# Cross-attention into a gated MLP on one Trainium2 core: one x load on another queue, the first output taken in pairs and partly ahead of the next scores, and fewer stores in the last group

## The chip, the core and the metric

The kernel runs on one core of a Trainium2 chip. The core has a matrix engine (TensorE, called PE in the profile, with its weight loads as PEld), three engines for elementwise work (VectorE = DVE, ScalarE = ACT, GpSimd = POOL) and SyncE (SP), which here only issues DMAs. PE writes to PSUM banks; DVE and ACT empty them into SBUF. DMAs are issued from the queues of SP, ACT and POOL. The metric is the time of one execution on the device, in microseconds; less is better.

## What is computed

The reference, cut to what matters:

```python
def _attn_ref(x, state):                      # x (8, 8, 512, 64), state (8, 8, 32, 64)
    scale = 1.0 / np.sqrt(D)
    scores = scale * np.matmul(x, state.transpose(0, 1, 3, 2))
    a = softmax(scores)                       # over the 32 state rows
    xread = np.matmul(a, state)
    scores2 = scale * np.matmul(state, x.transpose(0, 1, 3, 2))
    a2 = softmax(scores2)                     # over the 512 tokens
    sread = np.matmul(a2, x)
    return np.concatenate([xread, sread], axis=2)

def _moe_ref(x, w_gate, w_val, w_out):        # 512 -> 1536 -> 512
    gate = 1.0 / (1.0 + np.exp(-(x @ w_gate)))
    val = x @ w_val
    return (gate * val) @ w_out
```

The attention's 8 heads of 64 are joined to 512 columns, and every one of the 8 x 544 rows goes through the MLP. In the reference each softmax takes the maximum off first and adds 1e-9 to the sum; the kernel takes the exponential of the scaled scores alone.

## The kernel before

Work goes by batch: 8 batches of 512 tokens, and a ninth group of 256 rows that holds the 32 state rows of all batches (`b == B`). Matrix operands are bf16, sums fp32. xread is never formed: state times the gate and value weights (`SW`, by `sw_mm`) comes first, and the softmax weights, transposed (`aT`), multiply it.

For one batch the steps are these, each with its helper:

- `load_x` (L70): x of the batch, 1 MB of fp32, into one of three `xf` buffers. `cast_x` (L96) makes bf16 of it; from batch 2 on POOL does that.
- `at_xT_dma` (L121): four DMA transposes from SP's queue make `xT`.
- `S_mm` (L126), twice: 8 matmuls each, scores of half the heads into a PSUM bank. `S_exp` (L132): ACT's exponential, which frees that bank. `n_sum`, `n_mul` (L146, L167): sum, reciprocal and product on DVE. `aT_dma` (L190): four DMA transposes from SP's queue.
- `sw_wide` (L253), twice: 32 matmuls for half of the 1536 columns of SW of the batch, into OU, AT and four banks of SWP; `sw_cp` (L271) moves them to SBUF on ACT or DVE.
- `gv_mm` (L278), 12 times: gate and value of 128 columns into the two GV banks; `gv_th` (ACT's tanh) and `gv_glu` (DVE) make `glu`.
- `out_mm` (L308), 12 times: a token chunk c of 128 (four chunks) needs 12 matmuls against `wo`, in three groups of four (f0 = 0, 4, 8). After the third group ACT writes the bank to `res`, one of three buffers, and SP stores it.
- `sr_mm`, `sr_inv`, `sr_fin` (L199 to L224): the state rows' read, into `XS`.

The PSUM banks are named by pool: AT and OU have one bank each, GV two, SWP four.

The order on each engine is the order in which the helpers are called; there is no scheduler. Lines 349 to 568 hold a prologue, written out by hand: loads, batches 0 and 1 up to their `glu`, casts and transposes of x of batches 2 and 3. In it x of batches 0 and 1 is loaded on SP's queue, most weights on POOL's, x of batch 2 on POOL's (L490), then three loads of `wo` (L491 to L493), and x of batch 3 on ACT's queue (L502).

Then the loop of L570 runs b from 1 to 8 over twelve steps f. In step f the output group f of batch b - 1 and, if b > 1, gate and value f of batch b run on PE, and the scores, SW and state read of batch nb = b + 1 are spread between. `v, q` (L580) tell which half of SW and which place in it a step has. For b = 1 gate and value are done, so the steps hold output groups of batch 0 alone, in the two GV banks, and the scores of batch 2 stand ahead of all steps (L572 to L578). After the loop come two chunks of the ninth group, with four stores each (L322 to L324), and chunk 3 of batch 7 in three pieces (`out_last`, L326), whose last store ends the program.

Of the kernel before, what the change touches and what calls it, by code (L numbers as in the profile page):

```python
# [8 lines left out]
FP = mybir.dt.float32  # L9
# [7 lines left out]
def kernel(  # L17
# [14 lines left out]
    nc = tc.nc  # L32
    B, H, S, D = x.shape
    Ns = state.shape[2]
    SC = S + Ns
# [7 lines left out]
    wp = ctx.enter_context(tc.tile_pool(name="wp", bufs=1))  # L43
# [3 lines left out]
    fp = ctx.enter_context(tc.tile_pool(name="fp", bufs=3))  # L47
# [22 lines left out]
    def load_x(b, eng, parts=1, hold=None):  # L70
        xf = stg.tile((128, H, 4, D), FP, name="xf")
        if hold is not None:

            hold.memset(xf[:, 0, 0, 0:1], 0.0)
        v = x[b].rearrange("h (p c) d -> p h c d", c=4)
        n = H // parts
        for i in range(parts):
            eng.dma_start(xf[:, n * i:n * i + n], v[:, n * i:n * i + n])
        xfs[b] = xf
# [2 lines left out]
        src = (moe_w_gate, moe_w_val)[w].rearrange("(k p) n -> p k n", p=128)  # L82
        nc.gpsimd.dma_start((wg, wv)[w][:, :, lo:lo + n], src[:, :, lo:lo + n])  # L83

    def gate():

        nc.gpsimd.tensor_copy(pre[:, 1:2], xfs[1][:, 0, 0, 0:1])

    def cast_w(w, cp):
        cp((wg, wv)[w][:, :, 0:256], wfs[w])  # L90
# [1 line left out]
    def load_wo(q):  # L92
        nc.gpsimd.dma_start(wo[:, 4 * q:4 * q + 4],
                            moe_w_out.rearrange("(k p) n -> p k n", p=128)[:, 4 * q:4 * q + 4])

    def cast_x(b, cp, lo, n):  # L96
        if b not in xbs:
            xbs[b] = xp.tile((128, 4, H, D), BF, name="xb")
        cp(xbs[b].rearrange("p c h d -> p h c d")[:, lo:lo + n], xfs[b][:, lo:lo + n])  # L99
# [26 lines left out]
    def S_mm(b, i, place):  # L126
        ps = held["S", b, i] = place[0].tile((128, 4, 2, 2, Ns), FP, name="Sp", tag=place[1])
        for jj in range(2):
            for c in range(4):
                nc.tensor.matmul(ps[:, c, :, jj], xTs[b][:, 2 * i + jj, c], sTz[:, b, 2 * i + jj], start=True, stop=True)  # L130

    def S_exp(b, i):  # L132
        if b not in E1s:
            E1s[b] = ap_.tile((128, 4, 2, 4, Ns), FP, name="E1")
        nc.scalar.activation(E1s[b][:, :, :, 2 * i:2 * i + 2].rearrange("p c e j n -> p (c e) j n"),  # L135
                             held["S", b, i].rearrange("p c e j n -> p (c e) j n"), AF.Exp, scale=scale)
# [9 lines left out]
    def n_sum(b, i):  # L146
        rs = ap_.tile((128, 8, 2), FP, name="rs")
        nc.vector.tensor_reduce(rs, halfE(b, i), AX.X, ALU.add)  # L148
        ri = held["ri", b, i] = ap_.tile((128, 8, 2), FP, name="ri")
        nc.vector.reciprocal(ri, rs)  # L150
# [16 lines left out]
    def n_mul(b, i, eng):  # L167
        if b not in abs_:
            abs_[b] = ap_.tile((128, 4, 2, 128), BF, name="ab")
        ri = held["ri", b, i]  # L170
        eng.tensor_tensor(abs_[b].rearrange("p c e (j n) -> p (c e) j n", n=Ns)[:, :, 2 * i:2 * i + 2], halfE(b, i),  # L171
                          ri.unsqueeze(3).to_broadcast((128, 8, 2, Ns)), ALU.mult)
# [17 lines left out]
    def aT_dma(b):  # L190
        for c in range(4):
            nc.sync.dma_start_transpose(aT_tile(b)[:, c], abs_[b][:, c].rearrange("p e k -> p (e k)"))
# [105 lines left out]
    def gv_glu(b, f):  # L298
        if b not in glus:
            glus[b] = fp.tile((128, NF, n_of(b)), BF, name="glu", bufs=2, padded_shape=(128, NF, 512))  # L300
        nc.vector.scalar_tensor_tensor(glus[b][:, f], held["th", b, f], 1.0, held["gv", b, f][1], ALU.add, ALU.mult)  # L301
# [5 lines left out]

    def out_mm(b, k):  # L308
        c, f0 = k // 3, (k % 3) * 4
        if f0 == 0:  # L310
            place = SWP if b == B else GV if b == 0 else OU
            ops[b, c] = place[0].tile((128, 512), FP, name="outp", tag=place[1])
        for f in range(f0, f0 + 4):
            nc.tensor.matmul(ops[b, c], glus[b][:, f, c * 128:(c + 1) * 128], wo[:, f],  # L314
                             start=(f == 0), stop=(f == NF - 1))
        if f0 == 8:
            res = fp.tile((128, 512), FP, name="res")
            nc.scalar.activation(res, ops[b, c], AF.Copy, scale=0.5)  # L318
            if b < B:
                nc.sync.dma_start(rows_of(b, c), res)  # L320
            else:
                for i in range(4):  # L322
                    r0 = (4 * c + i) * SC + S
                    nc.sync.dma_start(out[r0:r0 + Ns], res[i * Ns:(i + 1) * Ns])  # L324

    def out_last(b, c):  # L326

        res = fp.tile((128, 512), FP, name="res")
        for lo, n in ((0, 256), (256, 128), (384, 128)):
            cs = slice(lo, lo + n)  # L330
            ps = p_sw.tile((128, 512), FP, name="outp", tag="swp")[:, :n]
            for f in range(NF):
                nc.tensor.matmul(ps, glus[b][:, f, c * 128:(c + 1) * 128], wo[:, f, cs],  # L333
                                 start=(f == 0), stop=(f == NF - 1))
            if lo == 256:
                nc.scalar.activation(res[:, cs], ps, AF.Copy, scale=0.5)
                nc.scalar.dma_start(rows_of(b, c)[:, cs], res[:, cs])
            else:
                nc.vector.tensor_scalar(res[:, cs], ps, 0.5, None, op0=ALU.mult)
                nc.sync.dma_start(rows_of(b, c)[:, cs], res[:, cs])  # L340
# [8 lines left out]
    sf = wp.tile((128, 16, D), FP, name="sf")  # L349
    nc.sync.dma_start(sf, state.rearrange("b h (u l) d -> (b h u) l d", l=16))  # L350
    load_x(0, nc.sync, 2)
    load_x(1, nc.sync)
    wfs = []
    for src in (moe_w_gate, moe_w_val):
        wf = wp.tile((128, 4, 256), FP, name="wf", bufs=2)
        nc.sync.dma_start(wf, src.rearrange("(k p) n -> p k n", p=128)[:, :, 0:256])
        wfs.append(wf)
    make_identity(nc, ident)
    nc.vector.memset(sTz, 0.0)
    for e in range(2):  # L360
# [24 lines left out]
    def pad(b, n=1):  # L385
        for e in range(2):
            rows = slice(e * 64, (e + 1) * 64)
            nc.gpsimd.tensor_copy(sTz[rows, b:b + n, :, e], sTc[rows, b:b + n])

    cast_x(0, vec, 2, 2)  # L390
    cast_x(0, pool, 4, 2)
    cast_x(0, act, 0, 2)
# [11 lines left out]
    S_mm(0, 0, SWP)  # L404
    S_exp(0, 0)
    warm(12, SWP)
    gate()
    load_w(0, 256, 256)
    S_mm(0, 1, AT)
    cast_x(1, act, 4, 4)  # L410
# [80 lines left out]
    load_wo(0)  # L491
    load_wo(1)
    load_wo(2)  # L493
    gv_glu(0, 5)
    sw_cp(1, 512, 1, 1, vec)
    sw_visit(1, 512, 512, 0)
# [2 lines left out]
    sr_mm(1, AT)  # L499
    sw_cp(1, 512, 1, 0, vec)  # L500
    gv_mm(1, 1, GV)
    load_x(3, nc.scalar)  # L502
    gv_th(1, 1)
    sw_visit(0, 1024, 512, 0)
    sw_visit(0, 1024, 512, 1)
# [63 lines left out]

    for b in range(1, B + 1):  # L570
        nb = b + 1 if b + 1 < B else None
        if b == 1:  # L572
            for i in range(2):
                S_mm(nb, i, (AT, GV)[i])
                S_exp(nb, i)
                n_sum(nb, i)
                n_mul(nb, i, nc.vector)
            aT_dma(nb)  # L578
        for f in range(NF):
            v, q = f // 6, f % 6  # L580
            if nb is not None and q == 0:
                sw_wide(nb, v)
                sw_cp(nb, v, 0, 0, act)
                sw_cp(nb, v, 0, 1, act)
            for first in (nb is not None and q == 0, nb is None or q > 0):
                if first and b > 1:
                    gv_mm(b, f, SWP if b == B and f % 2 else GV)
                    gv_th(b, f)
                    gv_glu(b, f)
                elif not first and (b < B or f < 9):  # L590
                    out_mm(b - 1, f)
            if nb is not None:
                if q == 0:
                    sw_cp(nb, v, 1, 0, vec)
                elif q in (1, 3, 4):
                    k = {1: 3, 3: 4, 4: 5}[q]
                    sw_cp(nb, v, k // 2, k % 2, act)
                if f in (1, 2) and b > 1:
                    S_mm(nb, f - 1, AT)
                    S_exp(nb, f - 1)  # L600
                elif f in (6, 7):
                    n_tok(nb, f - 6)
                    if f == 7:
                        n_split(nb, 0)
                elif f == 8:
                    n_split(nb, 1)
                elif f == 9:
                    sr_mm(nb, AT)
                    sr_inv(nb)
                elif f == 10:  # L610
                    sr_fin(nb)
                if f in (2, 4) and b > 1:
                    n_sum(nb, f // 2 - 1)
                elif f in (3, 5) and b > 1:
                    n_mul(nb, f // 2 - 1, nc.vector)
                if f == 3:
                    at_Eb(nb)
                    if nb + 2 < B:
                        load_x(nb + 2, nc.sync)
                elif f == 5 and b > 1:  # L620
                    aT_dma(nb)
                    if nb + 1 < B:
                        cast_x(nb + 1, pool, 0, 4)
                        cast_x(nb + 1, pool, 4, 4)
                        at_xT_dma(nb + 1)
# [33 lines left out]
```

The softmax here doesn't subtract the row's maximum and nothing guards it: scores larger than these inputs give would overflow.

## Time and profile before

| what | us |
|---|---|
| median of 13 runs (lowest, highest) | 231.36 (230.74, 233.78) |
| the profiled execution's own time | 232.05 |
| its span, first to last instruction | 230.2 |
| PE busy in the span | 219.0 |
| DVE, ACT, POOL busy | 141.5, 131.3, 42.5 |
| x of batch 3, issue to landing | 15.6 |
| the three `wo` loads, issue to landing | 12.7, 16.8, 19.6 |

Times inside the span count from its start. A busy time is the union of an engine's instructions; a wait of one engine is put down to what ended it. The ends of matmuls are modelled, so distances between matmuls are best taken from start to start. In a timeline row the columns are start, length, engine, line, operation, what it writes and reads, shape, how many were merged, and in brackets the idle time before it with what ended it. "SPq" and "ACTq" are the DMA queues' issuing instructions. A DMA's landing is the time at which its completion shows.

### The profile page before, as it was taken

What the parts mean: (1) busy time and instruction counts of PE and PEld (TensorE: products, weight loads), DVE (VectorE), ACT (ScalarE), POOL (GpSimd) and SP (SyncE); (2) the same over time, 40 slices, a digit from 0 to 9 for tenths busy, and PEclk for the clock granted to TensorE, in tenths of its full rate; (3) what the DMA queues carried; (4) which work ended last, traced back from release to release, by engine and by line L of the source; (5) the groups of instructions that cost most, each with busy time, mean ns of one, the idle gap of its engine ahead of it and who ended that gap; (6) DMA issues with size and microseconds to landing.
All of it is one profiled execution on the core that took longest, in us unless ns stands there. A gap on an engine that the chain in (4) does not pass through costs nothing.

```text
span 230.2 us, 4759 instructions
## 1 busy us (share of the span) xinstructions
PE 219.0 (95%) x1856; PEld 113.0 (49%) x1856; DVE 141.5 (61%) x234; ACT 131.3 (57%) x246; POOL 42.5 (18%) x75
## 2 busy tenths in 40 slices
PE   7678999989899999999999999999999999999994
PEld 6563345444444444444444544454445444466744
DVE  2499889975339864886478747874687443332311
ACT  3587877655467566665675567655755544423311
POOL 1399820150006000600060006000200000000000
PEclk9889999999999999999999999999999999999999
DMA  6999999923658243724372441235122111111113
GB/s 214 354 154 195 227 272 241 176 49 80 163 215 257 54 80 114 231 80 81 117 217 85 82 126 46 68 75 133 46 65 74 47 46 48 47 69 67 49 30 107
DMA packets 38790, 28.09 MB, mean 122 GB/s; under 512 B 20976, under 2 KB 34160, under 8 KB 38768
## 3 DMA queue, kind: packets, MB, share of 16 engines
q1 hardware_dynamic: 32560, 21.44, 33.5%
q0 software_dynamic: 5024, 5.24, 12.9%
q10 hardware_dynamic: 1184, 1.11, 1.7%
q8 instruction: 14, 0.23, 0.4%
q14 instruction: 8, 0.07, 0.1%
HBM read 18.35 MB, written 8.91 MB: 118 GB/s over the span
## 4 chain that ended last, share of the span: by engine, by line
PE 77%; DMA 13%; SPq 3%; POOL 3%; ACT 1%; issue 1%; DVE 0%; POOLq 0%; ACTq 0%
PE outp L314 35%; PE gvp L286 29%; PE gvp L289 5%; PE swp L234 4%; DMA xf<-in_x_dram 4%; DMA wv<-in_moe_w_val_dram 4%; DMA out_dram<-res 4%; DMA xT<-xb 3%; SPq L124 2%; PE srp L211 1%; PE outp L333 1%; PE Sp L130 1%; POOL xb L99 1%; PE srp L208 1%; POOL wg L83 1%
## 5 line engine op out<-in xcount | busy, mean ns | idle before, releaser
L301 DVE SCALAR_TENSOR_TENSOR glu<-th,gvp 128x512 bf16<-128x512 f32 (+1 forms) x108 | 70.3, 657 | 65.4 <-ACT th L296 50.6
L314 PE MATMUL outp<-wo,glu 128*128 128x512 bf16 x396 | 97.7, 379 | 0.2 <-ACT res L318 0.2
L286 PE MATMUL gvp<-aT,SW 128*128 128x512 bf16 x384 | 96.4, 379 | 1.0 <-ACT res L318 0.9
L296 ACT ACTIVATE th<-gvp 128x512 f32<-128x512 f32 (+1 forms) x108 | 61.6, 575 | 62.2 <-PE gvp L286 51.4
L286 PEld LDWEIGHTS <-SW 128*128 128x128 bf16 x384 | 36.2, 98 | 46.1 <-issue 5.2
L314 PEld LDWEIGHTS <-glu 128*128 128x128 bf16 x396 | 37.5, 98 | 41.4 <-issue 0.9
L272 ACT CAST SW<-swp 128x512 bf16<-128x512 f32 (+1 forms) x78 | 42.2, 578 | 3.0 <-PE swp L234 1.6
L318 ACT ACTIVATE res<-outp 128x512 f32<-128x512 f32 x33 | 19.7, 597 | 21.3 <-PE outp L314 17.5
L141 POOL CAST Eb<-E 128x256 bf16<-128x256 f32 x32 | 12.4, 429 | 99.3 <-ACT E L135 99.3
L99 POOL CAST xb<-xf 128x1024 bf16<-128x1024 f32 (+1 forms) x13 | 14.6, 1147 | 21.5 <-DMA xf<-in_x_dram 16.5
L272 DVE CAST SW<-swp 128x512 bf16<-128x512 f32 x20 | 13.4, 684 | 2.9 <-PE swp L234 2.9
L171 DVE TENSOR_TENSOR ab<-E,ri 128x512 bf16<-128x512 f32 x14 | 13.9, 989 | 0.1
L156 DVE TENSOR_REDUCE E<-E 128x128 f32<-128x512 f32 x12 | 12.3, 1032 | 0.0
L234 PE MATMUL swp<-wg,sTc 64*32 64x256 bf16 (+1 forms) x256 | 11.8, 328 | 0.2 <-ACT E L135 0.2
L234 PEld LDWEIGHTS <-sTc 64*32 64x32 bf16 x512 | 6.2, 90 | 10.8 <-issue 7.6
L148 DVE TENSOR_REDUCE rs<-E 128x16 f32<-128x512 f32 x16 | 10.8, 677 | 0.9 <-ACT E L135 0.9
L234 PE MATMUL swp<-wv,sTc 64*32 64x256 bf16 (+1 forms) x256 | 10.5, 324 | 0.5 <-DMA wv<-in_moe_w_val_dram 0.3
L135 ACT ACTIVATE E<-Sp 128x512 f32<-128x512 f32 x16 | 9.6, 609 | 1.8 <-PE Sp L130 1.8
L130 PE MATMUL Sp<-sTz,xT 128*128 128x64 bf16 x128 | 7.0, 199 | 1.7 <-ACT xT L119 0.6
L130 PEld LDWEIGHTS <-xT 128*128 128x128 bf16 x128 | 6.1, 102 | 4.8 <-DMA xT<-xb 0.9
L216 DVE RECIPROCAL r<-srp 128x128 f32<-128x128 f32 x8 | 7.6, 951 | 1.1 <-PE srp L211 1.1
L347 PE MATMUL warm<-ident 128*128 128x128 bf16 x56 | 6.1, 297 | 1.4 <-POOL ident masks.py:199 1.4
(53 smaller groups left out, 103.8 us busy)
## 6 DMA issues: line engine op xcount, KB each, us to landing
out_dram<-res SPq DMA_DIRECT2D x31, 256.0 KB, 2.5
xf<-in_x_dram SPq DMA_DIRECT2D x5, 1024.0 KB, 6.5
wo<-in_moe_w_out_dram POOLq DMA_DIRECT2D x3, 512.0 KB, 16.8
xf<-in_x_dram SPq DMA_DIRECT2D x2, 512.0 KB, 5.8
wg<-in_moe_w_gate_dram POOLq DMA_DIRECT2D x2, 512.0 KB, 7.5
wv<-in_moe_w_val_dram POOLq DMA_DIRECT2D x2, 512.0 KB, 8.6
xf<-in_x_dram POOLq DMA_DIRECT2D x1, 1024.0 KB, 9.7
xf<-in_x_dram ACTq DMA_DIRECT2D x1, 1024.0 KB, 15.6
```

Of the source, the lines that this page charges most:

```text
L99: cp(xbs[b].rearrange("p c h d -> p h c d")[:, lo:lo + n], xfs[b][:, lo:lo + n])
L130: nc.tensor.matmul(ps[:, c, :, jj], xTs[b][:, 2 * i + jj, c], sTz[:, b, 2 * i + jj], start=True, stop=True)
L141: nc.gpsimd.tensor_copy(Ebs[b][:, c], E1s[b][:, c])
L156: nc.vector.tensor_reduce(held["E4", b][:, e].rearrange("p j n -> p (j n)"), E1s[b][:, :, e].rearrange("p c j n -> p (j n) c"), AX.X, ALU.add)
L171: eng.tensor_tensor(abs_[b].rearrange("p c e (j n) -> p (c e) j n", n=Ns)[:, :, 2 * i:2 * i + 2], halfE(b, i), ri.unsqueeze(3).to_broadcas ...
L234: nc.tensor.matmul(pss[e][j * Ns:(j + 1) * Ns, o:o + n], sTc[rows, b, j], (wg, wv)[w][rows, j, lo:lo + n], start=True, stop=True)
L272: cp(*sw_left.pop((b, lo, w, e)))
L286: nc.tensor.matmul(ps, SWs[b][:, g, w, fs], aTs[b][:, :, g], start=(g == 0), stop=(g == 1))
L296: nc.scalar.activation(th, held["gv", b, f][0], AF.Tanh, scale=0.5)
L301: nc.vector.scalar_tensor_tensor(glus[b][:, f], held["th", b, f], 1.0, held["gv", b, f][1], ALU.add, ALU.mult)
L314: nc.tensor.matmul(ops[b, c], glus[b][:, f, c * 128:(c + 1) * 128], wo[:, f], start=(f == 0), stop=(f == NF - 1))
L318: nc.scalar.activation(res, ops[b, c], AF.Copy, scale=0.5)
```

## The change

- x of batch 3 is loaded on POOL's queue, after the `wo` loads, instead of on ACT's.
- The output groups of batch 0 run in pairs of chunks: for chunks 0 and 1 f0 = 0, then 4, then 8 of both, then the same for chunks 2 and 3. Before, chunk after chunk.
- The scores of batch 2 stand after output groups 0 and 1 of batch 0 instead of ahead of all; the second half of the scores uses OU, not GV. The first wide SW group of batch 2 comes at step 3 instead of 0, the second at step 6 as before, and their copies close up.
- x of batch 4 is loaded at step 6 instead of 3, and the last step of the state read of batch 2 stands one step earlier.
- `res` has four buffers instead of three.
- A chunk of the ninth group has one store, of four pieces of 32 rows, instead of four stores.
- The calls that load x of batch 1 and the first weights stand a few lines lower, and two helpers take an argument.

```diff
-    def gate():
-
-        nc.gpsimd.tensor_copy(pre[:, 1:2], xfs[1][:, 0, 0, 0:1])
+    def gate(landed):
+
+        nc.gpsimd.tensor_copy(pre[:, 1:2], landed)
+
+    def load_wf(w):
+        wfs[w] = wp.tile((128, 4, 256), FP, name="wf", bufs=2)
+        nc.sync.dma_start(wfs[w], (moe_w_gate, moe_w_val)[w].rearrange("(k p) n -> p k n", p=128)[:, :, 0:256])
...
     def out_mm(b, k):
         c, f0 = k // 3, (k % 3) * 4
+        if b == 0:
+
+            c, f0 = k // 6 * 2 + k % 2, k % 6 // 2 * 4
...
-            res = fp.tile((128, 512), FP, name="res")
+            res = fp.tile((128, 512), FP, name="res", bufs=4)
             nc.scalar.activation(res, ops[b, c], AF.Copy, scale=0.5)
             if b < B:
                 nc.sync.dma_start(rows_of(b, c), res)
             else:
-                for i in range(4):
-                    r0 = (4 * c + i) * SC + S
-                    nc.sync.dma_start(out[r0:r0 + Ns], res[i * Ns:(i + 1) * Ns])
+                nc.sync.dma_start(out.rearrange("(b s) d -> b s d", s=SC)[4 * c:4 * c + 4, S:SC], res)
 
     def out_last(b, c):
 
-        res = fp.tile((128, 512), FP, name="res")
+        res = fp.tile((128, 512), FP, name="res", bufs=4)
...
     load_x(0, nc.sync, 2)
-    load_x(1, nc.sync)
-    wfs = []
-    for src in (moe_w_gate, moe_w_val):
-        wf = wp.tile((128, 4, 256), FP, name="wf", bufs=2)
-        nc.sync.dma_start(wf, src.rearrange("(k p) n -> p k n", p=128)[:, :, 0:256])
-        wfs.append(wf)
+    wfs = {}
...
+    load_x(1, nc.sync)
+    load_wf(0)
+    load_wf(1)
     cast_x(0, vec, 2, 2)
...
     load_wo(2)
+    load_x(3, nc.gpsimd)
...
-    load_x(3, nc.scalar)
...
     for b in range(1, B + 1):
         nb = b + 1 if b + 1 < B else None
-        if b == 1:
-            for i in range(2):
-                S_mm(nb, i, (AT, GV)[i])
-                S_exp(nb, i)
-                n_sum(nb, i)
-                n_mul(nb, i, nc.vector)
-            aT_dma(nb)
         for f in range(NF):
-            v, q = f // 6, f % 6
+
+            v, q = divmod(f, 6) if b > 1 else (0, f - 3) if f < 6 else (1, f - 6)
             if nb is not None and q == 0:
                 sw_wide(nb, v)
...
             if nb is not None:
                 if q == 0:
                     sw_cp(nb, v, 1, 0, vec)
-                elif q in (1, 3, 4):
-                    k = {1: 3, 3: 4, 4: 5}[q]
+                if b == 1 and f == 1:
+                    for i in range(2):
+                        S_mm(nb, i, (AT, OU)[i])
+                        S_exp(nb, i)
+                        n_sum(nb, i)
+                        n_mul(nb, i, nc.vector)
+                    aT_dma(nb)
+                for k in ({1: (3,), 3: (4,), 4: (5,)} if b > 1 else {0: (3,), 1: (4, 5)}).get(q, ()):
                     sw_cp(nb, v, k // 2, k % 2, act)
...
                     sr_mm(nb, AT)
                     sr_inv(nb)
-                elif f == 10:
+                    if b == 1:
+                        sr_fin(nb)
+                elif f == 10 and b > 1:
                     sr_fin(nb)
...
-                if f == 3:
+                if g == 3:
                     at_Eb(nb)
-                    if nb + 2 < B:
-                        load_x(nb + 2, nc.sync)
-                elif f == 5 and b > 1:
+                if nb + 2 < B and f == (6 if b == 1 else 3):
+                    load_x(nb + 2, nc.sync)
+                if g == 5 and b > 1:
                     aT_dma(nb)
```

The rest of the diff writes `g`, which equals f, for f in the conditions of the later batches.

More of the change, by code (lines that the diff above doesn't have):

```diff
@@ L406 @@
     warm(12, SWP)
-    gate()
+    gate(xfs[1][:, 0, 0, 0:1])
     load_w(0, 256, 256)
@@ L584 @@
                 sw_cp(nb, v, 0, 1, act)
-            for first in (nb is not None and q == 0, nb is None or q > 0):
+            ahead = nb is not None and q == 0
+            for first in (ahead, not ahead):
                 if first and b > 1:
@@ L594 @@
                     sw_cp(nb, v, 1, 0, vec)
-                elif q in (1, 3, 4):
-                    k = {1: 3, 3: 4, 4: 5}[q]
-                    sw_cp(nb, v, k // 2, k % 2, act)
[L598 to L601, printed above, removed]
+                if b == 1 and f == 1:
[6 more added lines that the diff above has]
+                for k in ({1: (3,), 3: (4,), 4: (5,)} if b > 1 else {0: (3,), 1: (4, 5)}).get(q, ()):
+                    sw_cp(nb, v, k // 2, k % 2, act)
+                g = f
+                if g in (1, 2) and b > 1:
+                    S_mm(nb, g - 1, AT)
+                    S_exp(nb, g - 1)
+                if f in (6, 7):
                     n_tok(nb, f - 6)
@@ L609 @@
                     sr_inv(nb)
-                elif f == 10:
+                    if b == 1:
+                        sr_fin(nb)
+                elif f == 10 and b > 1:
                     sr_fin(nb)
[L612 to L615, printed above, removed]
-                if f == 3:
+                if g in (2, 4) and b > 1:
+                    n_sum(nb, g // 2 - 1)
+                elif g in (3, 5) and b > 1:
+                    n_mul(nb, g // 2 - 1, nc.vector)
+                if g == 3:
                     at_Eb(nb)
-                    if nb + 2 < B:
-                        load_x(nb + 2, nc.sync)
-                elif f == 5 and b > 1:
+                if nb + 2 < B and f == (6 if b == 1 else 3):
+                    load_x(nb + 2, nc.sync)
+                if g == 5 and b > 1:
                     aT_dma(nb)
+                if f == 5 and b > 1:
                     if nb + 1 < B:
```

## The prediction

> **What bounds the kernel now.** I read the busy time by stretch first, since TensorE (PE) is busy for 219.0 of 230.2 us and the question is where the other 11.2 us lie. By stretches of ten microseconds 3.68 and 2.11 us of PE idle time lie in the first two and 2.9 behind 220, where the last results leave. Between 70 and 220 there is none: PE is the bound and other engines have slack. What is left stands here (columns: stretch, length, busy time of each engine with its instructions, granted clock, DMA share, GB/s):
>
> ```profile
> 44.00:46.00 2.00, 1.94 (x11) 0.84 (x9) 1.74 (x3) 1.47 (x3) 0.77 (x1) 1.00 1.35 145
> 46.00:48.00 2.00, 1.37 (x31) 0.84 (x39) 1.00 (x2) 1.00 (x3) 1.25 (x2) 1.00 0.00 1
> 48.00:60.00 12.00, 12.00 (x130) 5.68 (x115) 7.86 (x14) 6.88 (x14) 1.89 (x4) 1.00 0.40 82
> 60.00:62.00 2.00, 1.91 (x37) 0.72 (x36) 0.46 (x2) 0.00 (x0) 0.00 (x0) 1.00 0.67 173
> 62.00:64.00 2.00, 1.20 (x6) 0.55 (x6) 0.00 (x0) 1.85 (x4) 0.00 (x0) 1.00 0.97 286
> ```
>
> The reader is to see two holes, at 46 to 48 and at 62 to 64. Busy time hides part of them (ends of matmuls are modelled), so I measure them by starts in the timeline. The first:
>
> ```profile
> 45.23 2.02 POOL L99 CAST xb<-xf 128x1024 bf16<-128x1024 f32 x2 [10.16 <-DMA xf<-in_x_dram]
> 45.69 0.25 PE L130 MATMUL Sp<-sTz,xT 128*128 128x64 bf16 x2
> 46.64 0.55 PE L130 MATMUL Sp<-sTz,xT 128*128 128x64 bf16 x13 [0.28 <-DMA xT<-xb]
> 47.06 1.08 ACT L135 ACTIVATE E<-Sp 128x512 f32<-128x512 f32 x2 [1.00 <-PE Sp L130]
> 47.70 0.41 PE L234 MATMUL swp<-wg,sTc 64*32 64x512 bf16 x7 [0.20 <-ACT E L135]
> 48.48 0.82 PE L314 MATMUL outp<-wo,glu 128*128 128x512 bf16 x3
> ```
>
> The scores of batch 2 come to PE before their transposed x has landed (46.59), and the wide SW group then waits for the exponential to free AT. From S_mm's start to the first output matmul it is 2.79 us. In the next batch eight score matmuls hold PE for 0.23 us (89.87 to 90.10) and a wide SW group 0.78 (85.63 to 86.41), so the work is 2 x 0.23 + 0.78 = 1.24: lost 1.55 us. The second hole:
>
> ```profile
> 62.15 0.60 ACT L318 ACTIVATE res<-outp 128x512 f32<-128x512 f32 x1 [3.25 <-DMA out_dram<-res]
> 62.80 0.59 PE L286 MATMUL gvp<-aT,SW 128*128 128x512 bf16 x2 [0.89 <-ACT res L318]
> 63.28 1.89 PE L314 MATMUL outp<-wo,glu 128*128 128x512 bf16 x8
> 67.78 0.60 ACT L318 ACTIVATE res<-outp 128x512 f32<-128x512 f32 x1 [0.57 <-DMA out_dram<-res]
> 68.43 1.02 PE L314 MATMUL outp<-wo,glu 128*128 128x512 bf16 x4 [0.21 <-ACT res L318]
> ```
>
> ACT can't empty the GV bank since all three res buffers wait for their stores. gv_mm holds PE from 61.30 to 63.28, in the next batch 0.87 (86.41 to 87.28): lost 1.11. The score group at 67.83 takes 0.60 where 0.23 is usual: lost 0.37. Why the stores are late, SyncE's queue tells:
>
> ```profile
> 35.09 18.03 SPq L124 DMA_TRANSPOSE xT<-xb  x8
> 53.23 5.05 SPq L192 DMA_TRANSPOSE aT<-ab  x4
> 58.38 0.53 SPq L320 DMA_DIRECT2D out_dram<-res  x1
> 58.95 0.43 SPq L78 DMA_DIRECT2D xf<-in_x_dram  x1
> 59.48 9.26 SPq L320 DMA_DIRECT2D out_dram<-res  x4
> ```
>
> Result 0 is ready at 51.88 and leaves at 58.38, behind the transposes of batch 3, which wait for the POOL cast at 45.23 and so for x of batch 3 (landed 45.1, 15.6 us after its issue). The three holes hold 1.55 + 1.11 + 0.37 = 3.03 us.
>
> **x of batch 3 on POOL's queue, last.** One DMA issue leaves ACT (0.43 us at 29.52) and one of 0.90 (the row of x of batch 2) comes to POOL at 26.3. Behind it there pad(2, 6) slides from 28.06 to 28.96; its reader is S_mm at 45, so 16 us of cover; without it 0.9 us. The queue it passes to holds gate and value weights, x of batch 2 and three wo loads. Alone in that queue, wg and wv of 512 KB landed 2.6 us apart (27.4, 30.0) and x of batch 2 2.9 later (32.9). At that pace wo lands at 35.5, 38.1, 40.7 (now 36.8, 41.6, 45.15 against x of batch 3 on ACT's queue; between 33 and 39 us the two queues moved 729 and 666 packets side by side) and x of batch 3 at 43.6. The transposes of batch 2 share the engines: from 32.9 to 46.6 these moved three wo (7.8), an x (2.9) and four transposes, which leaves 3.0 for the latter. So x lands between 43.6 and 46.6; I take 44.5, since from 40 to 41.5 us the three queues were served packet for packet (about 160 each), and a transpose's packets are small: most of them come after the loads.
>
> The Trainium skill (Trainium Kernel Development and Optimization, Key Constraints) says that queues of SP, ACT and POOL run on the same 16 DMA engines, and that issuing from several saves only issue time. By it this edit brings x of batch 3 at 45.1 as now, and the sum below stays the same, because 45.1 still meets its need.
>
> That need: cast, transposes of xT and aT take from landing to last aT landing 59.42 - 45.10 = 14.3 us. At 44.5 the queue is free for aT(2) at 52.6, at 45.1 at 53.2; aT lands 58.8 or 59.4.
>
> **Output of batch 0 ahead of the scores.** Nothing is added on PE, 8 matmul groups of four (0.865 each: 1.73 for two in the batch after) change place. Starts now: groups 0 and 1 at 45.69 and 46.55 (GV banks free at 45.20 by tanh and 45.92 by DVE; wo is there), scores 47.42 and 47.65 (xT at 46.6 by the worst of now), group 2 at 47.88 to 48.74. First new wait: OU now holds scores, so the wide group needs the second exponential: 47.82 + 1.08 = 48.90, wait 0.2. Queued behind: all of PE. Wide group to 49.72, groups 3, 4, 5 to 52.31. Second new wait: both chunks end close together, so ACT has res (0.60), two SW casts (1.07; from res start to their end 1.56 in the row at 51.28) from 51.65 to 53.21, and the next wide group's third part, due at 52.75, needs their banks: 0.5. Bounds of the two: 0 if ACT's order keeps up, 1.55 if the old hole comes back whole; I take 0.7, from these rows. Also on DVE, n_mul of batch 2 ends 48.45 + 3.4 = 51.9 (now 51.1), before the queue is free: nothing. load_x(4) goes behind two stores: lands 6.6 after 58, its cast is at 70.8: nothing, with 6 us of cover. sr_fin one group sooner: DVE is idle there.
>
> PE then has 12 x 0.865 + 0.46 + 2 x 0.78 + 0.69 (srp group) = 13.1, plus 0.7: the wide group of batch 3 at 59.5, gv_mm at 60.3, output at 61.1, where now it is 63.28.
>
> **Loads at the front.** load_x(1) and the two wf loads stand later in the text, yet SyncE gets nothing between, so its order is the same: no cost. In the built order each SyncE DMA waits for the one eight places before it, and with the ACT issue gone all shift by one; the first store then waits for a transpose of batch 3, landed six us before: nothing.
>
> **Four res buffers, stores earlier.** aT's issue ends near 57.7, the first two stores follow; result 0 of batch 1 needs only the first one's buffer, landed by 62 (3.67 us in the busy queue now), while ACT wants it near 65.5. The 1.11 and the 0.37 go. What's late next is nothing: aT lands 58.8 to 59.4, PE needs it at 60.3, margin 0.9 to 1.5.
>
> **One store per chunk in the last group.** Six issues of 0.4 us leave SyncE:
>
> ```profile
> 222.53 4.31 SPq L324 DMA_DIRECT2D out_dram<-res  x8
> 226.94 0.88 SPq L340 DMA_DIRECT2D out_dram<-res  x2
> 227.15 0.29 DVE L339 TENSOR_SCALAR res<-outp 128x128 f32<-128x128 f32 x1 [0.91 <-PE outp L333]
> ```
>
> The very last store starts at 227.47, right after its DVE copy, so freeing the queue gains nothing at the end. A store of four pieces is in no row. Ends: a plain 256 KB store lands in 2.0 to 2.3 us, then 225.12 + 2.3 is well ahead of the last landing, 229.16: cost 0; four 64 KB stores at 1.7 in series, 6.8 us: landing 231.9, cost 2.8. I take 0.3, near the plain row, of which it has the size.
>
> The Trainium skill (DMA: Bandwidth & Descriptors, Why a DMA increments its semaphore by 16 and not by 1) says that a DMA uses the largest number of engines up to 16 that divides both slowest dimensions. Here they are 4 and 128, so 4 engines; no run here shows it, and it speaks against the edit: an estimate from it is 32 rows an engine instead of 8, and the last two stores queued behind them, 0.2 to 0.5 us.
>
> **Sum.** Holes 3.03, new waits -0.7, last store -0.3: 2.0 us less. The profiled execution took 232.05 with a span of 230.2; it becomes about 230.0 with 228.2. The median shown is 231.36, so 229.4.
>
> **Rivals.**
> A. Half of it: ACT's longer queue and the OU wait give back the first hole (1.55 in place of 0.7) and the 0.37 stays. Then 3.03 - 1.55 - 0.37 - 0.3 = 0.8: 230.6. For it: ACT is where both new waits end; against: its rows have 0.49 us between starts and it sits idle 1.4 us before each result.
> B. The last store sets the end: 2.8 instead of 0.3 gives 231.9. For it: it's the only operation that no row shows; against: a plain store of its size would land at 227.4, 1.7 us before it matters.
> C. Slower: x of batch 3, served only after wo in one queue, comes late. If wo keeps its 45.15 and x's 1 MB goes at 512 KB per 2.6 us, it lands at 50.3, aT at 64.6, 4.3 after PE's 60.3: 231.36 - 2.0 + 4.3 = 233.7. It decides from a landing past 46.0, and eats the whole gain at 48.0. For it: wo took 19.6 us; against: without the other queue the weights went 2.6 us apart.
>
> **How the numbers follow.** Forecast 0.64, A 0.18, B 0.08, C 0.10. Under 0.5% (1.16 us) nothing can be told from no change, so faster is below 230.2, slower above 232.5. The forecast's own range is 228.8 (0.1 wait, free store) to 230.2; with A and part of B 228.8 to 231.3. Faster 0.65, same 0.25, slower 0.10.
>
> **What shows it.** PE going from the last gv_mm at 45.5 into output groups; 16 scores without a DMA wait; a wait of 0.2 and one of 0.5 ahead of the two wide groups; x of batch 3 landed between 43.6 and 46.6; aT(2) complete by 59.4; no ACT wait for a store near 62 and 67; the last two big stores landing within 4 us. I am wrong if x lands past 46.0, if the SW waits pass 1.5, or if the end stands over 3.5 us behind the last DVE copy (2.8 now).

## The result, and the profile after

The changed kernel takes 233.81 us (median of 11 runs, 232.95 to 235.70); the kernel before, run beside it, 231.55 (48 runs, 229.84 to 233.81). The ratio is 1.0101, with a 95% interval of 1.0074 to 1.0128: slower by 1%. The prediction of 229.4 us, and its range up to 231.3, is wrong, and so is its direction (it had said faster). The profiled execution took 234.79 with a span of 233.0 (230.2 before).

First the busy time by stretch of the changed kernel, the same stretches as before (columns: stretch, length, PE, PEld, DVE, ACT and POOL busy, granted clock, DMA share, GB/s):

```profile
44.00:46.00 2.00, 2.00 (x11) 0.92 (x10) 1.65 (x4) 1.28 (x3) 0.00 (x0) 1.00 1.40 70
46.00:48.00 2.00, 1.70 (x10) 0.68 (x7) 0.53 (x1) 0.00 (x0) 1.11 (x2) 1.00 1.00 146
48.00:60.00 12.00, 11.45 (x137) 5.64 (x137) 8.20 (x14) 7.39 (x15) 2.80 (x5) 1.00 0.33 62
60.00:62.00 2.00, 1.62 (x37) 0.67 (x36) 0.47 (x2) 1.73 (x4) 0.00 (x0) 1.00 0.34 98
62.00:64.00 2.00, 2.00 (x11) 0.94 (x10) 0.99 (x2) 0.78 (x2) 0.00 (x0) 1.00 1.09 245
```

The holes at 46 to 48 (0.63 us of idle PE before) and at 62 to 64 (0.80) are smaller or gone. There are new, smaller ones at 48 to 60 and at 60 to 62. The timeline tells which (rows of PE, and one of POOL):

```profile
45.45 1.89 PE L321 MATMUL outp<-wo,glu 128*128 128x512 bf16 x8
46.89 2.02 POOL L103 CAST xb<-xf 128x1024 bf16<-128x1024 f32 x2 [11.17 <-DMA xf<-in_x_dram]
47.18 0.37 PE L134 MATMUL Sp<-sTz,xT 128*128 128x64 bf16 x2
47.84 0.20 PE L134 MATMUL Sp<-sTz,xT 128*128 128x64 bf16 x1 [0.30 <-DMA xT<-xb]
48.32 0.55 PE L134 MATMUL Sp<-sTz,xT 128*128 128x64 bf16 x13 [0.27 <-DMA xT<-xb]
48.71 1.03 PE L321 MATMUL outp<-wo,glu 128*128 128x512 bf16 x4
49.87 0.41 PE L238 MATMUL swp<-wg,sTc 64*32 64x512 bf16 x8
53.34 0.41 PE L238 MATMUL swp<-wg,sTc 64*32 64x512 bf16 x8
54.54 3.63 PE L321 MATMUL outp<-wo,glu 128*128 128x512 bf16 x16
60.52 0.43 PE L238 MATMUL swp<-wg,sTc 64*32 64x512 bf16 x8
61.76 1.02 PE L290 MATMUL gvp<-aT,SW 128*128 128x512 bf16 x4 [0.38 <-ACT SW L276]
62.62 1.89 PE L321 MATMUL outp<-wo,glu 128*128 128x512 bf16 x8
```

Output groups now run right behind the last `gv_mm`. The 16 score matmuls hold PE from 47.18 to 48.71, 1.53 us where 0.46 is work: their xT still lands too late. From 48.71 to 49.87 it is 1.16 for one output group of 0.865: 0.3 for the second exponential. The wide group at 53.34 takes 1.20 in place of 0.78 (0.42 lost). The one at 60.52 takes 1.24 (0.46 lost): aT of batch 2, issued until 60.52, has landed in full only at 61.66. The row at 61.76 names ACT, but the result of ACT that had held the GV bank ended by 61.22. `gv_mm` to output is 0.86 (61.76 to 62.62) where it was 1.98, so the second hole is gone. All in all PE has gained: the last DVE copy starts at 226.12, before at 227.15, 1.03 us sooner.

The loss stands behind that. The end of the timeline of the changed kernel:

```profile
221.51 3.13 SPq L329 DMA_DIRECT2D out_dram<-res  x2
225.24 1.54 SPq L345 DMA_DIRECT2D out_dram<-res  x2
226.12 0.29 DVE L344 TENSOR_SCALAR res<-outp 128x128 f32<-128x128 f32 x1 [0.92 <-PE outp L338]
```

Its stores by size (columns: count, size of one, median us to landing):

```profile
out_dram<-res SPq DMA_DIRECT2D x33, 256.0 KB, 2.5
out_dram<-res SPq DMA_DIRECT2D x1, 128.0 KB, 6.3
out_dram<-res ACTq DMA_DIRECT2D x1, 64.0 KB, 6.0
out_dram<-res SPq DMA_DIRECT2D x1, 64.0 KB, 5.5
```

The same of the kernel before, whose nine 64 KB stores on SP's queue are the eight of the ninth group and the last one:

```profile
out_dram<-res SPq DMA_DIRECT2D x9, 64.0 KB, 1.7
out_dram<-res SPq DMA_DIRECT2D x1, 128.0 KB, 2.0
out_dram<-res ACTq DMA_DIRECT2D x1, 64.0 KB, 1.7
```

The last three stores of the program, the pieces of `out_last`, take 6.3, 6.0 and 5.5 us to land; before, they took 2.0, 1.7 and 1.7. The very last lands at 231.94, which is 5.82 us behind the start of the last DVE copy; before it was 2.01 (227.15 to 229.16). So 3.8 us are lost at the end, 1.0 is gained before it, and the span grows by 2.8.

What is in the way is seen in the stretches in which almost nothing but the two stores of the ninth group (issued at 221.51 and 224.10) moves, again of the changed kernel:

```profile
224.00:225.00 1.00, 1.00 (x15) 0.93 (x14) 0.22 (x1) 0.07 (x1) 0.00 (x0) 1.00 0.18 45
225.00:226.00 1.00, 1.00 (x20) 0.91 (x17) 0.21 (x1) 0.28 (x1) 0.00 (x0) 1.00 0.24 94
```

The DMA share (last but one) is 0.24, a quarter of 16 engines: four work, twelve stand idle. The 256 rows of 2 KB of the two stores, most of them 84 ns long, begin between 222.8 and 230.8, eight microseconds for what four engines at that pace do in 5.4 (64 x 84 ns).

A DMA raises a counter, its semaphore, in steps as its data land, and the trace has the times of these steps. They show the same without the share. A store of the kernel before comes in sixteen steps. Each of these two has one step soon after its issue (222.59, 225.06) and then four: 226.90 to 227.75 for the first, 229.90 to 231.21 for the second. The very last store of the program has twelve of its sixteen steps by 229.57, and the other four at 230.72, 231.19, 231.73 and 231.94. So it waits for four engines, on which the two large stores still have rows.

### The profile page after: what moved, and what is told of

Read it like the earlier page. It is cut to its first block, busy times and chain, and to the rows that moved or that the text cites. A ratio compares the mean times of both kernels' runs of the same rounds, so it can differ in the third digit from the quotient of the medians.

```text
span 233.0 us, 4753 instructions
## 1 busy us (share of the span) xinstructions
PE 219.2 (94%) x1856; PEld 113.3 (49%) x1856; DVE 141.4 (61%) x234; ACT 131.3 (56%) x246; POOL 43.5 (19%) x76
## 4 chain that ended last, share of the span: by engine, by line
PE 75%; DMA 11%; POOL 5%; SPq 3%; ACT 2%; issue 1%; DVE 0%; POOLq 0%; ACTq 0%
PE outp L321 35%; PE gvp L290 27%; DMA xf<-in_x_dram 8%; PE gvp L293 5%; PE swp L238 4%; DMA xT<-xb 3%; SPq L128 2%; PE srp L215 1%; PE Sp L134 1%; POOL Eb L145 1%; PE outp L338 1%; POOL wg L83 1%; POOL ab L175 1%; POOL xb L103 1%; ACT SW L276 1%
## 5 line engine op out<-in xcount | busy, mean ns | idle before, releaser
L293 PE MATMUL gvp<-XS,wg 128*128 128x256 bf16 x48 | 7.2, 273 | 0.0
```

Of the source, the lines that this page charges most:

```text
L293: nc.tensor.matmul(ps, (wg, wv)[w][:, j, fs], XS[:, j], start=(j == 0), stop=(j == 3))
```

## The experiments

Each ran beside the kernel before, whose median was 231.59 in the first group (E1 to E4), 231.47 in the second (E5 to E8) and 232.24 in the third (E9 to E11). Kernels of different groups are compared by their ratios to it.

### E1: the change with four stores per chunk

```diff
-                nc.sync.dma_start(out.rearrange("(b s) d -> b s d", s=SC)[4 * c:4 * c + 4, S:SC], res)
+                for i in range(4):
+                    r0 = (4 * c + i) * SC + S
+                    nc.sync.dma_start(out[r0:r0 + Ns], res[i * Ns:(i + 1) * Ns])
```

> The changed kernel with four stores per chunk of the ninth group again. Theory T (the single store per chunk holds up the last three stores; everything else in the change gains about 1 us): distance from the last DVE copy's start to the last landing goes back from 5.8 us to about 2.0, the median falls by 3 to 4 us against the changed kernel, to 230.0 to 230.8, some 1 us under the kernel before. Rival R (the loss comes from the moved x load or the new order, and the late stores only show it): the median stays at 233 or above and over the kernel before.

Measured: 229.97 us (8 runs, 229.69 to 230.50), ratio 0.9917 [0.9885, 0.9948]. The last store lands 2.03 us behind the start of the last DVE copy (225.04 to 227.07). This one part turns the change from a loss into a gain of 1.6 us by the medians, 1.9 by the ratio. Its PE timeline, and the last DVE copy:

```profile
47.23 0.25 PE L134 MATMUL Sp<-sTz,xT 128*128 128x64 bf16 x3
47.67 0.55 PE L134 MATMUL Sp<-sTz,xT 128*128 128x64 bf16 x13 [0.19 <-DMA xT<-xb]
48.05 1.03 PE L321 MATMUL outp<-wo,glu 128*128 128x512 bf16 x4
49.22 0.41 PE L238 MATMUL swp<-wg,sTc 64*32 64x512 bf16 x8
60.66 1.04 PE L290 MATMUL gvp<-aT,SW 128*128 128x512 bf16 x4
225.04 0.29 DVE L346 TENSOR_SCALAR res<-outp 128x128 f32<-128x128 f32 x1 [0.92 <-PE outp L340]
```

Here the scores lose 0.36 (47.23 to 48.05, less 0.46), the exponential 0.3, the SW banks 0.42 (52.69 to 53.89), and aT nothing: it landed at 60.20, ahead of 60.66. Together 1.08; 3.03 - 1.08 = 1.95, and the span is 228.2 against 230.2.

### E2: the kernel before with one store per chunk

The edit is the last `dma_start` of the diff above put into the kernel before, and nothing else.

> The kernel before with one store per chunk as the only edit. T: PE's last matmul stays where it was (227.1), the last landing comes 5 to 6 us after the last DVE copy instead of 2.0, and the median rises by 3.3 to 4.3 us, to about 235.3. R: within 0.5 us of the kernel before.

Measured: 235.18 us (4 runs), ratio 1.0146 [1.0096, 1.0197]; 5.78 us from the last DVE copy (226.53) to the last landing (232.31), and the last three stores took 6.3, 5.9 and 5.5 us, as in the changed kernel within 0.1. The store alone costs 3.6 us by the medians.

### E4: one store per chunk, the 32 rows outermost

```diff
-            nc.vector.tensor_tensor(XS[rows, :, b * Ns:(b + 1) * Ns], sr[rows, :, e], r2[rows], ALU.mult)
+            to = XS[rows, :, b // 4 * 128:b // 4 * 128 + 128].rearrange("p j (n b) -> p j n b", b=4)[:, :, :, b % 4]
+            nc.vector.tensor_tensor(to, sr[rows, :, e], r2[rows], ALU.mult)
...
-                nc.sync.dma_start(out.rearrange("(b s) d -> b s d", s=SC)[4 * c:4 * c + 4, S:SC], res)
+                nc.sync.dma_start(out.rearrange("(b s) d -> s b d", s=SC)[S:SC, 4 * c:4 * c + 4], res)
```

The state rows are laid out row by row instead of batch by batch, so the same 256 KB leave in one store of the same 2 KB rows, but with 32 as the outermost size in place of 4.

> The changed kernel with one store per chunk whose outermost dimension is the 32 state rows and not the 4 batches; the columns of XS are laid out to match, the same 128 pieces of 2 KB go to the same places. Theory K (the outermost sizes, 4 and 128, leave the store on 4 of 16 DMA engines): with 32 and 128 it runs on 16, each big store lands in 2.0 to 2.5 us, the last landing comes about 2.0 us after the last DVE copy, median 230.0 to 230.8. Rival P (a store in pieces is slow whatever the order): last landing 5 us or more after the copy, median 233.5 to 234.

Measured: 230.79 us (10 runs), ratio 0.9970 [0.9941, 1.0000]. The two stores landed in 2.49 and 2.40 us, and the last landing of all is 1.93 us behind the start of the last DVE copy. The same stretches as above, of this kernel:

```profile
224.00:225.00 1.00, 1.00 (x15) 0.93 (x14) 0.24 (x1) 0.05 (x1) 0.00 (x0) 1.00 0.00 0
225.00:226.00 1.00, 1.00 (x20) 0.89 (x16) 0.19 (x1) 0.28 (x1) 0.00 (x0) 1.00 0.70 258
```

The first store is over by 224; the second moves at 258 GB/s, where the changed kernel has 94. So neither the size of a store nor its scattered target rows makes it slow, but the outermost size. The kernel is 0.8 us above E1 all the same. Writing XS in this layout made that DVE operation 443 ns long instead of 288, 16 times in all. Behind two of them, at 41.43, PE waits 0.58 us for DVE (its row at 43.11), where E1 has no wait; whether this is the larger part of the 0.8 was not tried.

### E9 to E11: which store, and how many pieces

The changed kernel with these lines in place of its one store. E11, shown here, has n = 2: two stores of two pieces in each chunk. E9 has `4 if c == 0 else 1`, so the first chunk alone has one store and the second four; E10 has `4 if c == 1 else 1`, the second chunk alone.

```diff
+                n = 2
+                for i in range(0, 4, n):
+                    nc.sync.dma_start(out.rearrange("(b s) d -> b s d", s=SC)[4 * c + i:4 * c + i + n, S:SC], res[i * Ns:(i + n) * Ns])
```

> The kernel with four stores per chunk (229.97), but the first chunk of the ninth group has one store of four pieces, the second keeps four. Theory (one outer block of 32 rows after another on a quarter of the engines: 128 rows of 2 KB, four at a time, 84 ns each, 2.7 us, after a slow start of 1.5 us seen in the changed kernel): issued 221.5, its packets run from 222.7 to 227, so the later stores meet it with about 1 to 2 us left on four engines: 230.2 to 231.5, last landing 2.3 to 3.5 us behind the start of the last DVE copy (2.03 with four stores, 5.82 in the changed kernel). Rival (only the last of the two stores counts, the first is out of the way): 229.8 to 230.1, 2.0 us.

> The second chunk alone has one store of four pieces. Theory: issued near 223.2, packets from 224.4 for 2.7 to 4.2 us to 227.1 to 228.6, then what of the last three stores lies on the same engines: last landing 3.0 to 4.5 us behind the start of the last DVE copy (2.03 with four stores), 231.0 to 232.5. Rival (the two stores hold up only each other): as with four stores, 229.8 to 230.2.

> Each chunk has two stores of two pieces of 32 rows. Theory (the number of pieces sets how many engines a store runs on, so two): 64 rows an engine for each pair, 5.4 us a chunk at least if both stores get the same two engines: last landing 6 to 11 us behind the start of the last DVE copy, 234 to 239; if the two stores get different engines, as the changed kernel's: 5 to 6.5 us, 233 to 234.5. Rival (it is the size of one store that makes it late, 256 KB against 64): half of the changed kernel's loss, last landing 3.5 to 4.5 us behind, 231.3 to 232.5.

| kernel | median us (runs) | ratio [95%] | last landing behind the start of the last DVE copy, us |
|---|---|---|---|
| E1, four stores each | 229.97 (8) | 0.9917 [0.9885, 0.9948] | 2.03 |
| E9, one for the first chunk | 230.68 (10) | 0.9945 [0.9910, 0.9979] | 2.78 |
| E10, one for the second | 233.38 (10) | 1.0052 [1.0017, 1.0086] | 4.80 |
| the change, one for each | 233.81 (11) | 1.0101 [1.0074, 1.0128] | 5.82 |
| E11, two of two pieces each | 238.03 (5) | 1.0239 [1.0169, 1.0309] | 11.07 |

Both stores count, the second for most of it (2.8 of 3.8 us by the traces). E9 lies within its theory's range; E10 lies above it (4.80 where 3.0 to 4.5 was expected). E11 decides against size: its stores are half as large, and the end is 5 us later still (its profiled execution, 240.73 us, is the slowest of its five; by the ratios it is 3.2 us over the change). The stretches of its tail:

```profile
226.00:227.00 1.00, 0.94 (x17) 0.76 (x14) 0.08 (x2) 0.28 (x1) 0.00 (x0) 1.00 0.12 37
230.00:232.00 2.00, 0.00 (x0) 0.00 (x0) 0.00 (x0) 0.00 (x0) 0.00 (x0) 0.50 0.14 33
232.00:234.00 2.00, 0.00 (x0) 0.00 (x0) 0.00 (x0) 0.00 (x0) 0.00 (x0) 0.50 0.12 45
234.00:236.00 2.00, 0.00 (x0) 0.00 (x0) 0.00 (x0) 0.00 (x0) 0.00 (x0) 0.50 0.13 51
```

A share of 0.12 to 0.14 is two engines of 16. At 226 to 227 it is no more, though three of the four stores are issued (at 222.35, 223.09 and 224.94, the fourth from 225.50 to 226.76) and none has landed: they stand on the same two. The semaphore steps agree: each store comes in two steps behind its first one, and they land one behind another, at 227.75, 231.19, 234.96 and 237.52. The very last store of the program has fourteen of its sixteen steps by 230.46, and the other two at 237.05 and 238.04. So two pieces take two engines, four pieces four, and 32 outermost all sixteen (E4's two stores come in sixteen steps each, as E1's stores of 32 rows do).

### E3: the change with four stores and x of batch 3 on ACT's queue

```diff
     load_wo(2)
-    load_x(3, nc.gpsimd)
...
     gv_mm(1, 1, GV)
+    load_x(3, nc.scalar)
```

> As the four-store version, with x of batch 3 on ACT's queue again. Theory X (behind wo on POOL's queue x of batch 3 and with it the transposes of batch 2 land 1.5 us later than before): x of batch 3 lands at about 45.1, xT of batch 2 by 46.7, the scores of batch 2 run without a wait of over 0.3 us, aT of batch 2 lands by 59.5, and the median is 0.8 to 1.5 us under the four-store version. Rival Y (the POOL queue brings it no later; what differed was that one execution): within 0.4 us of the four-store version.

Measured: 229.77 us (9 runs), ratio 0.9921 [0.9892, 0.9949], level with E1 (229.97), as rival Y had it: with the output ahead of the scores, the queue of this load is worth nothing that can be told. Theory X does not hold: x of batch 3 lands at 44.72, but the last `wo` at 46.68, and xT of batch 2 is complete only at 48.11.

### E5, E6, E7: one part of the change each

E5 is the kernel before with `bufs=4` for `res` (both places); E6 is E3 with three buffers, so the new order (and the small moves of the change) alone; E7 is the kernel before with x of batch 3 on POOL's queue.

> The kernel before with four res buffers as the only edit. Theory B (the hole at 62 us is the lack of a fourth buffer, and with it goes): no wait of ACT for a store near 62 and 67 us, output group 0 of batch 1 starts 0.9 us or less after gv_mm of batch 2, median 0.9 to 1.5 us under the kernel before (230.0 to 230.7). Rival (another wait takes its place there, as PE then runs into aT of batch 2): within 0.5 us of the kernel before.

> The new order of batch 0's output alone: four stores per chunk, x of batch 3 on ACT's queue, three res buffers. Theory O (the order gains on its own by covering the wait for xT of batch 2): 0.3 to 0.9 us under the kernel before, and 0.7 to 1.5 over the same version with four buffers (229.8), since the hole at 62 us stays. Rival (the pairs end two chunks late and close together, so three buffers hold up ACT more than before): slower than the kernel before.

> The kernel before with x of batch 3 on POOL's queue behind wo as the only edit. Theory N (the 16 DMA engines are full until 45 us, so the queue only changes which load is late): x of batch 3 lands between 44.5 and 47, xT of batch 2 not before 46, median within 0.6 us of the kernel before. Rival (it comes too late for aT of batch 2): 0.7 to 2 us slower.

E5: 230.79 us (12 runs), ratio 0.9972 [0.9937, 1.0008]. In its PE timeline the second hole is gone (0.87 from 61.14 to 62.01), and the first stands, 3.19 us from 45.12:

```profile
45.12 0.20 PE L130 MATMUL Sp<-sTz,xT 128*128 128x64 bf16 x1
48.31 5.35 PE L314 MATMUL outp<-wo,glu 128*128 128x512 bf16 x24
61.14 1.04 PE L286 MATMUL gvp<-aT,SW 128*128 128x512 bf16 x4
62.01 1.89 PE L314 MATMUL outp<-wo,glu 128*128 128x512 bf16 x8
```

E6: 230.93 us (12 runs), ratio 0.9959 [0.9930, 0.9988]. Of the buffer wait one remains: ACT's result at 61.36 has waited 0.97 for a store, and `gv_mm` holds PE 1.15 (61.34 to 62.49). So each of the two is worth 0.5 to 0.7 us by the medians, 0.65 and 0.95 by the ratios, where E5's interval still includes no gain; both together, E3, 1.8. E5 gains less than theory B had said.

E7: 232.95 us (12 runs), ratio 1.0052 [1.0020, 1.0083], slower by 1.5 us by the medians, 1.2 by the ratio. That size had been expected of aT; the trace shows another wait. Its stretches:

```profile
44.00:46.00 2.00, 1.46 (x7) 0.49 (x5) 1.65 (x4) 1.19 (x2) 0.00 (x0) 1.00 1.49 41
46.00:48.00 2.00, 0.76 (x8) 0.45 (x9) 0.38 (x1) 0.00 (x0) 1.64 (x2) 1.00 0.61 120
48.00:50.00 2.00, 1.81 (x45) 0.94 (x42) 0.97 (x3) 1.60 (x4) 0.98 (x3) 0.76 0.20 40
50.00:52.00 2.00, 2.00 (x19) 0.67 (x6) 1.93 (x4) 1.05 (x3) 1.30 (x3) 0.50 0.58 99
52.00:54.00 2.00, 2.00 (x10) 0.88 (x9) 0.90 (x2) 0.00 (x0) 0.00 (x0) 0.88 0.34 66
```

PE's output groups behind that wait:

```profile
50.24 6.44 PE L314 MATMUL outp<-wo,glu 128*128 128x512 bf16 x24
```

The scores at the head of PE's queue wait for xT (landed 46.41 to 47.80; before, complete at 46.59), PE is busy for 0.76 of the two microseconds from 46 on, and from 49.06 to 52.47 the granted clock is 0.50. The 24 output matmuls behind take 6.44 us where E5 has 5.35. aT landed at 60.55, and `gv_mm`, which needs it, comes behind the wide group that starts at 63.35: no wait.

How the 1.2 to 1.5 us divide between the late xT and the clock is not shown. The clock is hardly most of it: of the twelve executions the four with the lowest mean clock (0.978 to 0.985, the profiled one among them) are the slowest, but the other eight (0.990 and more) still have a median of 232.63, 1.2 above the kernel before. When the clock fell in those is not on record. Nor does a PE as idle as that always lose its clock: in E11's profile it is busy for 1.15 us of 46 to 48 and 0.81 of 48 to 50, and the clock stays at 1.00. In the changed kernel PE has output groups to do at that time, and its clock is 1.00 in every stretch from 44 to 64.

### E8: E3 without the two new waits

```diff
-                        S_mm(nb, i, (AT, OU)[i])
+                        S_mm(nb, i, (AT, SWP)[i])
...
-                for k in ({1: (3,), 3: (4,), 4: (5,)} if b > 1 else {0: (3,), 1: (4, 5)}).get(q, ()):
+                for k in ({1: (3,), 3: (4,), 4: (5,)} if b > 1 else {0: (3, 4, 5)}).get(q, ()):
```

> From the version with four stores and x of batch 3 on ACT's queue: the second half of batch 2's scores in a bank of SWP instead of OU, and ACT's two late SW copies of batch 2 directly behind its first one, ahead of the result's. Theory W (the two new PE waits ahead of the wide SW groups, 0.3 and 0.4 us, come from OU and from ACT's order): wide groups 0.80 us or less from start to the output group behind, median 0.3 to 0.8 us under that version (229.0 to 229.5). Rival (the time went to the landing of aT and comes back there as a wait): within 0.2 us of it.

Measured: 229.55 us (6 runs, 228.50 to 229.79), ratio 0.9880 [0.9836, 0.9924]. PE's rows show both waits gone:

```profile
48.54 1.03 PE L321 MATMUL outp<-wo,glu 128*128 128x512 bf16 x4
49.49 0.41 PE L238 MATMUL swp<-wg,sTc 64*32 64x512 bf16 x8
50.27 2.76 PE L321 MATMUL outp<-wo,glu 128*128 128x512 bf16 x12
52.96 0.41 PE L238 MATMUL swp<-wg,sTc 64*32 64x512 bf16 x8
53.74 3.63 PE L321 MATMUL outp<-wo,glu 128*128 128x512 bf16 x16
```

The output group takes 0.95 to the next start, each wide group 0.78. It is 0.22 us under E3 by the medians and 0.95 by the ratios, whose intervals overlap: whether the 0.3 to 0.8 came about can't be told. It has the lowest median measured here, 1.2% under the kernel before.

## Why the prediction was wrong

**One store per chunk: the step that failed.** The prediction says: "cost 0; four 64 KB stores at 1.7 in series, 6.8 us: landing 231.9, cost 2.8. I take 0.3, near the plain row, of which it has the size." Measured: 3.8 us at the end of the trace, 3.6 by E2's median, and between E1 and the change 3.8 by the medians and 4.3 by the ratios ((1.0101 - 0.9917) x 231.6). So it is a term of the sum taken near the wrong end, and even the far end was too near, as it let only one store count: 2.8 is what the second store alone costs (E10). Rival B, held at 0.08, has the right place with that price. The choice "by size" was the error: in E4 the same size costs nothing at the end, and in E11 half the size costs more.

The rule that spoke against the edit was at hand. The Trainium skill (DMA: Bandwidth & Descriptors, Why a DMA increments its semaphore by 16 and not by 1) gives four engines for outer sizes of 4 and 128, and the share of 0.24, the four steps of each landing and E11 agree. The estimate of 0.2 to 0.5 drawn from it went wrong in the working: it counted 32 rows an engine, those of one store alone. The same section says that a hardware queue's DMA takes the lowest-numbered engines. Which numbers they have no run here shows, but E11's share and its landings one behind another agree that such stores stand on the same engines. Then two stores stand on the same four, 64 rows in series, 5.4 us at 84 ns each, and each 16-engine store behind them has a share there and lands only when those four come to it, as the last steps of its landing show. As an estimate from these rows, with the first at 222.8, the two stores alone would take until 228.2, where with stores as before everything would have landed at 228.13 (226.12 + 2.01). What the last three stores have on these engines comes on top, and the rows in fact begin until 230.8.

**The three holes, 3.03 us.** Right: they are there and the change works on them. E5 removes the second and third; with the new order the first, 1.55, shrinks to 0.36 at the scores in E1 and to 1.07 in the changed kernel.

**The two new waits, 0.2 and 0.5.** Right: 0.3 and 0.42. E8 removes both, with one edit aimed at each.

**x of batch 3 "between 43.6 and 46.6; I take 44.5".** Wrong for the profiled execution: it landed at 46.77, past the 46.0 named as the point of decision. In seven profiled executions with the load on POOL's queue (the change, E1, E4, E7, E9, E10, E11) it landed at 44.8 to 48.1, on average 46.2: five of the seven within the stated range, all later than 44.5. In six with it on ACT's (before, E2, E3, E5, E6, E8) at 43.5 to 45.1, on average 44.2. In the changed kernel the first two `wo` loads kept the pace of 2.6 us (36.0, 38.6), but the third took 5.0 more (43.57): at 44 to 46 the DMA moved 70 GB/s at a share of 1.40 (the times of packets overlap, so a share can pass 1), where 40 to 41 had 362. The pace of a queue in its middle was carried to its end, and there it didn't hold.

The rule weighed there, one set of engines for all queues (the Trainium skill, Trainium Kernel Development and Optimization, Key Constraints), comes off better than the step: x later and `wo` sooner, and the last landing of the two kinds is at 46.0 on average with ACT's queue (x 45.10 and `wo` 45.15 before, `wo` 46.68 in E3) and 46.2 with POOL's. xT of batch 2 is complete 1.4 to 1.6 us behind whichever of the two is last, in all thirteen profiled executions (at 46.4 or later, mostly at 47 to 48). So the scores can wait with either queue (1.2 us in E6 and E8, with ACT's): "xT at 46.6 by the worst of now" was not the worst. In the changed kernel that cost 1.07 us at the scores and, since x was late, 0.46 at `gv_mm` for aT, as the prediction's condition has it. That is rival C's place at a tenth of its price; its landing at 50.3 was never reached. In E1 it was 0.36 and nothing.

**Four res buffers, nothing for loads at the front.** Right: no wait of ACT for a store near 62 and 67, and `gv_mm` to output in 0.86.

**The sum.** Without the store it would have been 3.03 - 1.08 = 1.95 (E1's trace) for a predicted 2.3; E1's median gives 1.6, its ratio 1.9. So the order and the buffers were worth most of what was said: 229.97 lies between the forecast and rival A, whose price for the new waits (1.55) was too high and whose 0.37 did not stay. Of the signals named two came true, x past 46.0 and an end over 3.5 us behind the last DVE copy. From the copy's end to the span's end it was 2.8 before and is 6.6 (226.42 to 233.0).

## What to carry to other kernels

Before merging stores, look at the outermost size of the merged access pattern: with four pieces there four DMA engines did all the work here, with two pieces two, and every later store waited for them. Two chunks with four small stores each, 32 rows outermost, beat two with one store of four pieces each by some 4 us. At the end of a program, where nothing hides a landing, such a term has to be priced by the row nearest in shape, not in size. Work that does not depend on a late load is worth placing ahead of what does: E7, where the load came late and nothing stood ahead, lost 1.2 to 1.5 us; E1, with the same queue, lost nothing against E3.

## What the runs showed of the hardware

- The number of pieces outermost set the DMA share: 0.12 to 0.14 with two, 0.24 with four, and 258 GB/s in the stretch with 32 (94 with four). The landings came in two, four and sixteen steps, and a store behind had its last two or four steps late (238.04 in E11, 231.94 in the changed kernel).
- The first store of four pieces started slowly: its seventeenth row began 1.45 us after its first (222.82, 224.27), later 16 rows began in 0.32. Why, no run tells.
- In E7's profile a PE busy for 0.76 of 2 us was followed by a granted clock of 0.50 from 49.06 to 52.47. That made a wait of 1.8 us dearer by another 1.1. In E11's, 0.81 of 2 us was followed by no change. What decides, no run tells.
- The tail of the load phase was slow: 70 GB/s at 44 to 46 with a DMA share of 1.40, and x of batch 3, last in POOL's queue, landed anywhere from 44.8 to 48.1 in seven kernels.
- DVE writing bf16 to every fourth element took 443 ns for 64x128 instead of 288.
